# Down products of a feed-forward block as pairs of 64-row matmuls, their token tiles changing halves of the array behind a semaphore

## The chip, the cores and the metric

The kernel runs on one core of a Trainium2 chip. The metric is the device time of one execution in microseconds. The engines are TensorE (PE; its weight loads are shown apart as PEld), VectorE (DVE), ScalarE (ACT), GpSimd (POOL) and SyncE (SP), which issues the DMAs.

## What is computed

```python
def _A_ref(x, wqkv, wo):                       # 32 heads of 18
    qkv = (x @ wqkv).reshape(B, S, 3, H, Dh).transpose(2, 0, 3, 1, 4)
    scores = einsum("bhqd,bhkd->bhqk", q, k) * (Dh ** -0.5)
    o = einsum("bhqk,bhkd->bhqd", softmax(scores), v)
    return o.transpose(0, 2, 1, 3).reshape(B, S, D) @ wo

def _B_ref(x, w_gate, w_up, w_down):
    return (gelu(x @ w_gate) * (x @ w_up)) @ w_down

xn = layernorm(x)                              # x: 1 x 2048 x 576, float32
return x + _A_ref(xn, wqkv, wo) * silu(_B_ref(xn, w_gate, w_up, w_down))   # F = 4608
```

## The kernel before

A matrix product of float32 numbers is made of three products of split parts: each operand is cut into a high part and the rest (`h` and `l` in the names), and high x high, high x low and low x high are summed.

The 2048 tokens are four blocks `b` of 512. The feed-forward part walks over 36 sections per token block, 144 in all; a section makes 128 of the 4608 hidden units for 512 tokens. Its 27 pairs of matmuls (`gate_up`, L422) work on 64 rows each: `pg` in the upper half of the array's rows, `pu` in the lower half. Between these pairs stand the attention's score matmuls, also as pairs of 64 rows: `pm` (L809, for the running maximum) and `pe` (L855, whose exponential is taken by ScalarE in L856). VectorE reduces each `pm` (L810). After a section of the attention's stretch come the values (`acc`, L872, 128 rows by 32 columns of weights), and then, after every second section, a down block.

A down block multiplies the gated hidden units of two sections (256 of them, as `G` = 2 groups) with their rows of `w_down`. From the sixth block on it does so by seven products in place of eight (a Strassen scheme, `PRODUCTS`): the operands `ah`, `al` (`A`, hidden units by tokens) and `T` (sums of parts of `w_down`) hold seven combinations, and each product is added into one of the seven accumulators `M` by VectorE (L545; for `r` = 0 it is a copy). The first five blocks (`PLAIN`) use the four plain products, of six terms each (`down_plain`, L525). A product writes `py`, a tile of two PSUM banks: bank `t` holds 128 tokens by 288 columns. In each bank the three terms are three matmuls of 128 rows and 288 columns, so a seven-product block is 42 matmuls and a plain one 48.

`ring("py")` takes the next of three PSUM buffers (`RING`) of two banks each. `pm`, `pe`, `acc`, `py` and, in some sections, `pgu` go through this same ring in the order of the program, so each allocation waits until the reader of the third tile ahead of it has ended.

The order on TensorE and SyncE is as written; on the other engines a scheduler sets it, apart from what is marked `keep_in_program_order`. Down blocks are called in `downs`, one section late: block k after section 2k + 2. The last three (`last_down`) are in the closing part, where TensorE is also busy with the output projection.

Of the kernel before, what the change touches and what calls it, by code (L numbers as in the profile page):

```python
# [17 lines left out]
P = 128  # L18
# [5 lines left out]
HR = 64  # L24
# [13 lines left out]
G = 2  # L38
NR = F // (G * P)
NF = NB * NR * G  # L40
# [5 lines left out]
DC, TH = D // 2, TB // 2  # L46
ENDS = NF - len(FIRST) - NU * NA
# [5 lines left out]
PRODUCTS = ((2, (0, 6)), (5, (1, 3)), (3, (2, 5)), (6, (3, 4)), (0, (4, 2)), (4, (5, 1)), (1, (6, 0)))  # L53
# [35 lines left out]
def kernel(ctx: ExitStack, tc: tile.TileContext, x, wqkv, wo, w_gate, w_up, w_down, out):  # L89
    nc = tc.nc  # L90
    x = x.rearrange("b s d -> (b s) d")
# [80 lines left out]
    with tc.tile_pool(name="pro", bufs=1) as pro, tc.tile_pool(name="pps", bufs=1, space=PSUM) as pps:  # L172
# [156 lines left out]
        t = ORDER[0]  # L329
# [24 lines left out]
        for b in range(NB):  # L354
# [41 lines left out]
    FF = {"w": ahead, "xd": XD, "down": [], "gates": [], "n": 0, "hooks": {}, "raw": {},  # L396
          "M": ffn.tile([P, 7, 2, DC], F32, name="M"),
          "A": [ffn.tile([P, 7, TH], F32R, name=m) for m in ("ah", "al")],
          "T": ffn.tile([P, 2, 7, DC], F32R, name="T")}
# [4 lines left out]
    def ring(name):  # L404

        return ps.tile([P, 2, TB], F32, name=name, tag="ring", bufs=RING)
# [104 lines left out]
    def cut_plain_b(raw):  # L511
        T = FF["T"]
        cut(T[:, 0, 0:4], T[:, 1, 0:4], raw.rearrange("p g (c d) -> p (g c) d", c=2), nc.scalar, nc.gpsimd,
            tc.keep_in_program_order)

    def down_plain():
        (ah, al), T, M = FF["A"], FF["T"], FF["M"]
        for i, c, into in ((0, 0, ((6, ALU.add),)), (0, 1, ((2, ALU.add), (5, ALU.subtract))),
                           (1, 0, ((3, ALU.subtract), (6, ALU.subtract))), (1, 1, ((5, ALU.add),))):
            py = ring("py")  # L520
            terms = [(h, 2 * g + i, w, 2 * g + c) for g in range(G) for h, w in ((ah, 0), (ah, 1), (al, 0))]
            for t in range(2):
                tt = slice(t * P, (t + 1) * P)
                for n, (h, a, w, k) in enumerate(terms):
                    nc.tensor.matmul(py[:, t, 0:DC], h[:, a, tt], T[:, w, k], start=n == 0, stop=n == len(terms) - 1)  # L525
            for m, op in into:
                nc.vector.tensor_tensor(M[:, m], M[:, m], py[:, :, 0:DC], op=op)

    def down(b, r, then={}):
        if b == 0 and r < PLAIN:  # L530
            return down_plain()
        (ah, al), T, M = FF["A"], FF["T"], FF["M"]
        for m, (i, k) in PRODUCTS:
            py = ring("py")
            for t in range(2):
                tt = slice(t * P, (t + 1) * P)
                for n, (h, w) in enumerate(((ah, 0), (ah, 1), (al, 0))):
                    nc.tensor.matmul(py[:, t, 0:DC], h[:, i, tt], T[:, w, k], start=n == 0, stop=n == 2)  # L538
            if r == 0:
                if b == 1:  # L540
                    nc.vector.tensor_copy(M[:, m], py[:, :, 0:DC])
                else:
                    nc.scalar.activation(M[:, m], py[:, :, 0:DC], AF.Copy)
            else:
                nc.vector.tensor_tensor(M[:, m], py[:, :, 0:DC], M[:, m], op=ALU.add)  # L545
            for eng, to, op, by in then.get(m, ()):
                eng.tensor_tensor(M[:, to], M[:, to], M[:, by], op=op)
        if r == NR - 1 and b < NB - 1:
            FF["gates"].append(b)
            for k, (p, q) in enumerate(COMBINED):  # L550
                combine_at(6 * k + 6, nc.gpsimd, q)
                combine_at(6 * k + 6, nc.gpsimd, p)

    def combine_at(i, eng, what):
        FF["hooks"].setdefault(i, []).append(lambda: combine(eng, *what))
# [65 lines left out]
    def downs(then={}):  # L621
        while FF["down"] and (FF["down"][0][-1] < FF["n"] or FF["n"] == NF):
            down(*FF["down"].pop(0)[:-1], then)
# [125 lines left out]
    with tc.tile_pool(name="att", bufs=1, reuse_waits="tile") as att:  # L749
# [179 lines left out]
        for n in range(NU * NA):  # L929
            u, i = divmod(n, NA)  # L930
# [7 lines left out]
            if FF["n"] % G == 1 and SCALED <= n < NU * NA - 2 and 2 < FF["n"] % (NR * G) < NR * G - 2:  # L938
                done = scaled + gated
                if (scaled + 1) * NA + 4 < n:  # L940
                    jobs, k = (load_scale, scale, store_scale), scaled
                    scaled += 1
                else:
                    jobs, k = (load_gate, gate, store_gate), gated
# [20 lines left out]
    with tc.tile_pool(name="epi", bufs=1, reuse_waits="tile") as epi:  # L965
# [7 lines left out]
        n = 0  # L973
# [94 lines left out]
        def last_section(tag):  # L1068

            n = FF["n"]  # L1070
            FF["n"] += 1
            g = n % G
            pairs, pg, pu = gate_up(tag)
            hooks, FF["hooks"] = FF["hooks"], {}
            nxt = FF["raw"].pop(n + 1, None)
            if nxt:
                split_gu(nxt, 0)
                split_gu(nxt, 1)
            for t in spread(pairs, (), 1, hooks):
                t()  # L1080
            if nxt:
                split_gu(nxt, 2)
            FF["w"] = nxt
            h = ffn.tile([P, 3 + 3 * g, TH], F32, name=f"h{g}", bufs=2 - g)
            t1 = h[:, 0:2].rearrange("p a t -> p (a t)")

            def gelu():
                act.activation(t1, pg, AF.Square)
                vec.scalar_tensor_tensor(t1, t1, 1.0 / GC, pg, op0=ADD, op1=ALU.mult)
                act.activation(t1, t1, AF.Tanh, scale=GC * GS)  # L1090
                vec.scalar_tensor_tensor(t1, t1, 1.0, pg, op0=ADD, op1=ALU.mult)
# [16 lines left out]
        h, gelu = last_section("f")  # L1108
# [10 lines left out]
        h, gelu = last_section("ring")  # L1119
# [23 lines left out]
        for m in ("rawd", "tsum"):  # L1143
            t = ffn.tile([P, 2, D], F32, name="xxs", tag=m)
# [5 lines left out]
        h, gelu = last_section("ring")  # L1150
# [10 lines left out]
        M = FF["M"]  # L1161
# [17 lines left out]
        for i, c, m in QUARTERS:  # L1179
            t = ffn.tile([P, 2, DC], F32, name="tg", tag=("h0", "h1")[c], bufs=2 - c)  # L1180
# [34 lines left out]
```

## Time and profile before

| | |
|---|---|
| runs | 2544.12, 2545.7, 2547.68 us; median 2545.7 |
| profiled execution | span 2542.7 us (the profile gives its span alone) |
| TensorE matmuls | busy 2534.6 us (100% of the span), 20548 matmuls, granted clock 0.999 |
| TensorE weight loads | 1837.5 us (72%) |
| VectorE, ScalarE, GpSimd | 2092.2 us (82%), 1452.9 us (57%), 1620.2 us (64%) |
| chain that ended last | TensorE 97%, of which `py` L538 15% and `py` L525 1% |

In the profile's lines a form such as 64*128 64x512 is a weight tile of 64 rows by 128 columns and a moving operand of 64 rows by 512 columns. Starts of matmuls are recorded, their ends are modelled, and matmuls overlap: the distance between two starts tells what one of them takes from TensorE. In a timeline the columns are start, duration, engine, line, operation, tiles (out<-in), forms and count; what stands in brackets is the idle time of the engine ahead of the row and what ended it. In a list of waits they are total, number and longest, in us. In the chain they are start, length and what it was. A group's row gives its busy time, the mean of one in ns, and the idle time ahead with its causes.

### The profile page before, as it was taken

To read this page: it belongs to the slowest core of one execution; us is meant where nothing else is said; L and a number is where in the kernel's file an instruction comes from. 1 tells how busy PE (TensorE), PEld (TensorE's weight loads), DVE (VectorE), ACT (ScalarE), POOL (GpSimd) and SP (SyncE) were. 2 spreads that over 40 slices of the span, in tenths; PEclk is the share of its full clock that TensorE was granted. 3 is DMA by queue.
4 is the path that set the end of the run, shared out by engine and by line. 5 is a ranking of instruction groups with operands and counts; after the bars stand their busy time and mean duration, and the time that the engine had idled before them with its cause. 6 is when DMAs were issued, how large, how long until landed. Compare 5 with 4: busy or idle time off the path is not lost.

```text
span 2542.7 us, 53140 instructions
## 1 busy us (share of the span) xinstructions
PE 2534.6 (100%) x20548; PEld 1837.5 (72%) x20548; DVE 2092.2 (82%) x2371; ACT 1452.9 (57%) x1753; POOL 1620.2 (64%) x1684
## 2 busy tenths in 40 slices
PE   9999999999999999999999999999999999999999
PEld 8888866667766676666667666776666676667689
DVE  5327888889888888888897898998898888888357
ACT  3223466666666665556666555655566665556621
POOL 3005688888888876666658565666667666666773
PEclk9999999999999999999999999999999999999999
DMA  8965465555685565667787777666668666665676
GB/s 259 312 207 136 117 176 158 163 162 164 168 252 147 165 173 146 167 163 166 172 221 187 172 167 169 172 169 164 155 158 236 167 172 173 164 168 154 190 188 236
DMA packets 416627, 455.04 MB, mean 179 GB/s; under 512 B 109428, under 2 KB 289396, under 8 KB 416376
## 3 DMA queue, kind: packets, MB, share of 16 engines
q1 hardware_dynamic: 416376, 451.64, 66.3%
q8 instruction: 164, 2.69, 0.5%
q14 instruction: 87, 0.71, 0.1%
HBM read 354.38 MB, written 97.13 MB: 178 GB/s over the span
## 4 chain that ended last, share of the span: by engine, by line
PE 97%; DVE 1%; POOL 1%; issue 0%; DMA 0%; ACT 0%; SPq 0%; DVEq 0%; POOLq 0%
PE pg L422 25%; PE acc L872 18%; PE py L538 15%; PE pm L809 9%; PE pe L855 9%; PE pu L422 9%; PE po L193 6%; PE po L1026 2%; PE pgu L422 2%; PE py L525 1%; PE pt L263 0%; POOL M L560 0%; DVE KA L756 0%; DMA xx<-in_A_x_dram 0%; DMA KA<-qk 0%
## 5 line engine op out<-in xcount | busy, mean ns | idle before, releaser
L856 ACT ACTIVATE pT<-pe 128x1024 f32<-128x1024 f32 x1024 | 1048.2, 1027 | 580.3 <-PE pe L855 544.5
L810 DVE TENSOR_REDUCE mx<-pm 128x2 f32<-128x1024 f32 x1024 | 1219.4, 1224 | 162.3 <-PE pm L809 145.7
L422 PE MATMUL pu<-xd,wh 64*128 64x512 f32 x2466 | 901.7, 396 | 0.0
L422 PE MATMUL pg<-xd,wh 64*128 64x512 f32 x2466 | 901.2, 396 | 0.0
L422 PEld LDWEIGHTS pg<-xd,wh 64*128 64x128 f32 x2466 | 454.5, 184 | 113.5 <-issue 55.4
L117 POOL TENSOR_SCALAR wh<-raw 128x384 fp32r<-128x384 f32 x402 | 211.8, 530 | 456.8 <-PE pu L422 275.3
L422 PE MATMUL pg<-xd,wl 64*128 64x512 f32 x1233 | 480.9, 390 | 0.3 <-POOL wl L124 0.3
L422 PE MATMUL pu<-xd,wl 64*128 64x512 f32 x1233 | 481.0, 390 | 0.0
L422 PEld LDWEIGHTS pu<-xd,wh 64*128 64x128 f32 x2466 | 454.3, 184 | 18.7
L872 PE MATMUL acc<-pT,VS 128*32 128x512 f32 x4096 | 466.0, 595 | 0.0
L119 POOL TENSOR_TENSOR wl<-raw,wh 128x384 fp32r<-128x384 f32 x402 | 422.4, 1054 | 26.4
L809 PE MATMUL pm<-KA,QT 64*128 64x512 f32 x2048 | 410.9, 393 | 0.4 <-ACT pT L856 0.3
L855 PE MATMUL pe<-QT,KA 64*128 64x512 f32 x2048 | 409.0, 391 | 0.3 <-DVE mx L810 0.3
L538 PE MATMUL py<-T,ah 128*128 128x288 f32 x1876 | 380.6, 298 | 0.0
L545 DVE TENSOR_TENSOR M<-py,M 128x576 f32<-128x576 f32 x448 | 338.8, 758 | 31.4 <-PE py L538 18.2
L538 PEld LDWEIGHTS py<-T,ah 128*128 128x128 f32 x1876 | 298.3, 188 | 54.0 <-issue 54.0
L451 POOL TENSOR_TENSOR al<-h,ah 128x512 fp32r<-128x512 f32 (+1 forms) x143 | 295.3, 2065 | 51.6 <-ACT ah L448 37.9
L872 PEld LDWEIGHTS acc<-pT,VS 128*32 128x32 f32 x4096 | 120.2, 109 | 276.6 <-issue 229.6
L538 PE MATMUL py<-T,al 128*128 128x288 f32 x938 | 275.6, 294 | 0.0
L855 PEld LDWEIGHTS pe<-QT,KA 64*128 64x128 f32 x2048 | 191.9, 184 | 110.8 <-DVE mx L810 25.5
L422 PEld LDWEIGHTS pg<-xd,wl 64*128 64x128 f32 x1233 | 227.3, 184 | 33.8 <-POOL wl L124 0.7
L422 PEld LDWEIGHTS pu<-xd,wl 64*128 64x128 f32 x1233 | 227.5, 185 | 10.4
(167 smaller groups left out, 2943.5 us busy)
## 6 DMA issues: line engine op xcount, KB each, us to landing
T<-ts SPq DMA_DIRECT2D x98, 576.0 KB
KA<-qk SPq DMA_DIRECT2D x768, 72.0 KB
T<-ts SPq DMA_DIRECT2D x98, 432.0 KB
raw<-in_B_w_gate_dram SPq DMA_DIRECT2D x144, 288.0 KB
raw<-in_B_w_up_dram SPq DMA_DIRECT2D x144, 256.0 KB
ts<-T SPq DMA_DIRECT2D x36, 576.0 KB
VS<-vs SPq DMA_DIRECT2D x128, 152.0 KB
qk<-t SPq DMA_DIRECT2D x72, 256.0 KB
```

The lines of the kernel that those rows point to most:

```text
L117: first = nc.gpsimd.tensor_scalar(hi, raw, 1.0, 1.0, op0=ALU.mult, op1=ALU.mult)
L119: keep(nc.gpsimd.tensor_tensor(lo, raw, f(hi), op=ALU.subtract))
L193: nc.tensor.matmul(o, st, m, start=(i == 0), stop=(i == len(terms) - 1))
L422: nc.tensor.matmul(o, w[1 + wp][k][rr, c, :], xd[k][xp][rr, c, :], start=(i == 0), stop=(i == len(terms) - 1))
L451: low = two.tensor_tensor(lo, raw, f(hi), op=ALU.subtract)
L538: nc.tensor.matmul(py[:, t, 0:DC], h[:, i, tt], T[:, w, k], start=n == 0, stop=n == 2)
L545: nc.vector.tensor_tensor(M[:, m], py[:, :, 0:DC], M[:, m], op=ALU.add)
L809: nc.tensor.matmul(pm[:, a], QS[u, r][rr, t * P:(t + 1) * P], KS[(u * NA + c) % KB][r][rr, :], start=True, stop=True)
L810: nc.vector.tensor_reduce(MX[u][:, 2 * r:2 * r + 2, t, c], pm, axis=AX.X, op=ALU.max)
L855: nc.tensor.matmul(pe[:, a], KS[(u * NA + c) % KB][r][rr, t * P:(t + 1) * P], QS[u, r][rr, :], start=True, stop=True)
L856: nc.scalar.activation(PT[u, kt][:, 2 * r:2 * r + 2, :], pe, AF.Exp, scale=SCALE)
L872: nc.tensor.matmul(ACC[u][32 * a:32 * a + 32, :], VS[(u * NA + c) % VB][:, v:v + 32], pt[:, a, :], start=first, stop=last, skip_group_chec ...
```

## The change

`halved` takes a list of products. Each product is done in two phases of 64-row matmuls. In phase 0 the upper 64 rows of the operands go to the first token tile (bank 0) while the lower 64 rows go to the second (bank 1); in phase 1 the token tiles change halves. So each bank gets all 128 rows, from one half of the array after the other. Phase 1 of a product stands behind phase 0 of the next product. The last matmul of phase 0 adds one to the semaphore `turns`, and the first of phase 1 waits for it.

All down blocks but those of the last sections use it: 68 of the 72, of which five are plain. The old loop stays for the other four.

```diff
+    def halved(jobs):
+        (ah, al), T = FF["A"], FF["T"]
+        begun = []
+
+        def phase(py, terms, x, turn=0):
+            for n, (h, a, w, k) in enumerate(terms):
+                for half in range(2):
+                    t, rr = half ^ x, slice(HR * half, HR * half + HR)
+                    one = nc.tensor.matmul(py[:, t, 0:DC], h[rr, a, t * P:(t + 1) * P], T[rr, w, k], start=x == 0 and n == 0,
+                                           stop=x == 1 and n == len(terms) - 1)
+                    if x == 1 and n == half == 0:
+                        one._wait_ge(turns, turn)
+            if x == 0:
+                TURN["n"] += 1
+                one.then_inc(turns, 1)
...
+        def turned():
+            py, terms, then, turn = begun.pop(0)
+            phase(py, terms, 1, turn)
+            then(py)
+
+        for n, (terms, then) in enumerate(jobs):
+            py = ring("py")
+            phase(py, terms, 0)
+            begun.append((py, terms, then, TURN["n"]))
+            if n > 0:
+                turned()
+        turned()
...
     def down(b, r, then={}):
...
-        for m, (i, k) in PRODUCTS:
-            py = ring("py")
-            for t in range(2):
-                tt = slice(t * P, (t + 1) * P)
-                for n, (h, w) in enumerate(((ah, 0), (ah, 1), (al, 0))):
-                    nc.tensor.matmul(py[:, t, 0:DC], h[:, i, tt], T[:, w, k], start=n == 0, stop=n == 2)
+        def take(py, m):
...
+        terms = ((ah, 0), (ah, 1), (al, 0))
+        if FF["n"] < NF - ENDS:
+            halved([([(h, i, w, k) for h, w in terms], lambda py, m=m: take(py, m)) for m, (i, k) in PRODUCTS])
+        else:
+            for m, (i, k) in PRODUCTS:
+                py = ring("py")
+                for t in range(2):
+                    tt = slice(t * P, (t + 1) * P)
+                    for n, (h, w) in enumerate(terms):
+                        nc.tensor.matmul(py[:, t, 0:DC], h[:, i, tt], T[:, w, k], start=n == 0, stop=n == 2)
+                take(py, m)
```

`down_plain` calls `halved` in the same way with its four products of six terms.

On TensorE, a seven-product block begins like this before (each `py` number is one product's tile; a wait for DVE_49 is one for VectorE):

```order
L538 MATMUL py_19123<-T_1917,ah_1915 128x288 [waits DMAHW1_49,PE_49]
L538 MATMUL py_19123<-T_1917,ah_1915 128x288 [waits DMAHW6_49]
L538 MATMUL py_19123<-T_1917,al_1916 128x288
L538 MATMUL py_19123<-T_1917,ah_1915 128x288 x2
L538 MATMUL py_19123<-T_1917,al_1916 128x288
L538 MATMUL py_19131<-T_1917,ah_1915 128x288 [waits DVE_49]
L538 MATMUL py_19131<-T_1917,ah_1915 128x288
L538 MATMUL py_19131<-T_1917,al_1916 128x288
```

On TensorE in the changed kernel, from the second product's first phase to the fourth's:

```order
L528 MATMUL py_19886<-T_1917,ah_1915 128x288 [waits DVE_49]
L528 MATMUL py_19886<-T_1917,ah_1915 128x288 x3
L528 MATMUL py_19886<-T_1917,al_1916 128x288 x2
L528 MATMUL py_19879<-T_1917,ah_1915 128x288 [waits turns]
L528 MATMUL py_19879<-T_1917,ah_1915 128x288 x3
L528 MATMUL py_19879<-T_1917,al_1916 128x288 x2
L528 MATMUL py_19900<-T_1917,ah_1915 128x288 [waits DVE_49,Pool_49]
...
L528 MATMUL py_19886<-T_1917,ah_1915 128x288 [waits turns]
...
L528 MATMUL py_19914<-T_1917,ah_1915 128x288 [waits DVE_49]
```

The first product (19879) is finished behind the first phase of the second (19886), and the fourth (19914), which takes the first one's buffer, begins six steps of two matmuls behind that, where twelve matmuls stood between them before.

On TensorE, a block's last rows in the changed kernel:

```order
L528 MATMUL py_19956<-T_1917,ah_1915 128x288 [waits DVE_49]
L528 MATMUL py_19956<-T_1917,ah_1915 128x288 x3
L528 MATMUL py_19956<-T_1917,al_1916 128x288 x2
L528 MATMUL py_19942<-T_1917,ah_1915 128x288 [waits turns]
L528 MATMUL py_19942<-T_1917,ah_1915 128x288 x3
L528 MATMUL py_19942<-T_1917,al_1916 128x288 x2
L528 MATMUL py_19956<-T_1917,ah_1915 128x288 [waits turns]
L528 MATMUL py_19956<-T_1917,ah_1915 128x288 x3
L528 MATMUL py_19956<-T_1917,al_1916 128x288 x2
```

The last two products end three steps apart, and the seventh waits for `turns` with only the sixth's second phase between. Every other matmul on TensorE stands in the same order as before, and SyncE's order is the same. The other engines run the same instructions; GpSimd's and ScalarE's order differs by a few places, and on VectorE the first addition of a plain block stands behind one activation step instead of ahead of it.

More of the change, by code (lines that the diff above doesn't have):

```diff
@@ L514, in cut_plain_b @@
             tc.keep_in_program_order)
+    turns = tc.alloc_semaphore("turns")
+    TURN = {"n": 0}
+    def halved(jobs):
[12 more added lines that the diff above has]
+                one.then_inc(turns, 1)
+                tc.no_tile_sem_insts.add(one.ins.name)
+                tc.add_to_no_dep_group(f"turn{TURN['n']}", one.ins)
+            else:
+                tc.declare_fence(one.ins, group=f"turn{turn}")
+        def turned():
[9 more added lines that the diff above has]
+        turned()
@@ L516, in down_plain, with add_to @@
     def down_plain():
-        (ah, al), T, M = FF["A"], FF["T"], FF["M"]
+        (ah, al), M = FF["A"], FF["M"]
+        jobs = []
         for i, c, into in ((0, 0, ((6, ALU.add),)), (0, 1, ((2, ALU.add), (5, ALU.subtract))),
                            (1, 0, ((3, ALU.subtract), (6, ALU.subtract))), (1, 1, ((5, ALU.add),))):
-            py = ring("py")
-            terms = [(h, 2 * g + i, w, 2 * g + c) for g in range(G) for h, w in ((ah, 0), (ah, 1), (al, 0))]
-            for t in range(2):
-                tt = slice(t * P, (t + 1) * P)
[L524 to L527, printed above, removed]
+            def add_to(py, into=into):
+                for m, op in into:
+                    nc.vector.tensor_tensor(M[:, m], M[:, m], py[:, :, 0:DC], op=op)
+            jobs.append(([(h, 2 * g + i, w, 2 * g + c) for g in range(G) for h, w in ((ah, 0), (ah, 1), (al, 0))], add_to))
@@ L529, in down @@
+        halved(jobs)
     def down(b, r, then={}):
@@ L532, in down @@
         (ah, al), T, M = FF["A"], FF["T"], FF["M"]
-        for m, (i, k) in PRODUCTS:
-            py = ring("py")
-            for t in range(2):
-                tt = slice(t * P, (t + 1) * P)
-                for n, (h, w) in enumerate(((ah, 0), (ah, 1), (al, 0))):
-                    nc.tensor.matmul(py[:, t, 0:DC], h[:, i, tt], T[:, w, k], start=n == 0, stop=n == 2)
+        def take(py, m):
             if r == 0:
@@ L547, in down @@
                 eng.tensor_tensor(M[:, to], M[:, to], M[:, by], op=op)
+        terms = ((ah, 0), (ah, 1), (al, 0))
+        if FF["n"] < NF - ENDS:
+            halved([([(h, i, w, k) for h, w in terms], lambda py, m=m: take(py, m)) for m, (i, k) in PRODUCTS])
+        else:
+            for m, (i, k) in PRODUCTS:
[5 more added lines that the diff above has]
+                take(py, m)
         if r == NR - 1 and b < NB - 1:
```

## The prediction

> **What bounds the kernel now.** I read the page first (busy shares and the chain that ended last), then the waits of TensorE, then the timeline of one down block on TensorE, its weight loads and VectorE.
>
> ```profile
> span 2542.7 us, 53140 instructions
> PE 2534.6 (100%) x20548; PEld 1837.5 (72%) x20548; DVE 2092.2 (82%) x2371; ACT 1452.9 (57%) x1753; POOL 1620.2 (64%) x1684
> PE 97%; DVE 1%; POOL 1%; issue 0%; DMA 0%; ACT 0%; SPq 0%; DVEq 0%; POOLq 0%
> PE pe L855 <- DVE mx L810: 0.3, 1, 0.3
> PE pm L809 <- ACT pT L856: 0.3, 1, 0.3
> PE pg L422 <- POOL wl L124: 0.3, 1, 0.3
> ```
>
> TensorE is the chain for 97%, and the three waits shown are one of 0.3 us each. Any time that TensorE gains or loses therefore shows in full. The next view is one down block (42 matmuls) between the values and the next section.
>
> ```profile
> 1003.48 0.53 PE L538 MATMUL py<-T,ah 128*128 128x288 f32 x2
> 1003.85 0.29 PE L538 MATMUL py<-T,al 128*128 128x288 f32 x1
> ...
> 1004.24 0.29 PE L538 MATMUL py<-T,al 128*128 128x288 f32 x1
> ...
> 1008.99 0.29 PE L538 MATMUL py<-T,al 128*128 128x288 f32 x1
> 1009.21 0.49 PE L422 MATMUL pg<-xd,wh 64*128 64x512 f32 x1
> ...
> 1009.55 0.40 PE L855 MATMUL pe<-QT,KA 64*128 64x512 f32 x2
> ...
> 1010.02 0.39 PE L809 MATMUL pm<-KA,QT 64*128 64x512 f32 x2
> ...
> 1010.72 0.40 PE L855 MATMUL pe<-QT,KA 64*128 64x512 f32 x2
> ...
> 1011.88 0.39 PE L855 MATMUL pe<-QT,KA 64*128 64x512 f32 x2
> ...
> 1019.08 0.39 PE L422 MATMUL pg<-xd,wh 64*128 64x512 f32 x1
> ```
>
> Starts matter here, since matmuls overlap. From the third matmul (1003.85) to the 42nd (1008.99) are 39 steps in 5.14 us: 0.132 us a step. From the second pair of the section (1009.55) to its 43rd (1019.08) are 41 pairs in 9.53 us: 0.232 us a pair of 512 columns. Between the last down matmul and the second pair lie 0.56 us where 0.132 + 0.232 = 0.36 would do: leaving the 128-row shape costs 0.20 us.
>
> VectorE beside it, with the means of its two largest jobs:
>
> ```profile
> 1004.57 0.76 DVE L545 TENSOR_TENSOR M<-py,M 128x576 f32<-128x576 f32 x1 [0.26 <-PE py L538]
> 1010.48 1.23 DVE L810 TENSOR_REDUCE mx<-pm 128x2 f32<-128x1024 f32 x1 [0.40 <-PE pm L809]
> L545 DVE TENSOR_TENSOR M<-py,M 128x576 f32<-128x576 f32 x448 | 338.8, 758 | 31.4 <-PE py L538 18.2
> ```
>
> The last matmul of the first product starts at 1004.24 and VectorE takes the product at 1004.57: 0.33 us, then 0.758 us. Seven takes need 5.3 us of the 42 x 0.132 = 5.5 us, so VectorE is nearly as full as TensorE there.
>
> What a late wait costs shows where the pm pair at 1756.46 waited for ScalarE:
>
> ```profile
> 1755.38 1.02 ACT L856 ACTIVATE pT<-pe 128x1024 f32<-128x1024 f32 x1 [2.31 <-PE pu L422]
> 1756.46 0.50 PE L809 MATMUL pm<-KA,QT 64*128 64x512 f32 x2
> 1756.79 0.40 PE L422 MATMUL pg<-xd,wh 64*128 64x512 f32 x1
> 1756.46 0.19 PEld L809 LDWEIGHTS pm<-KA,QT 64*128 64x128 f32 x2 [0.27 <-ACT pT L856]
> 1756.57 0.19 PEld L422 LDWEIGHTS pg<-xd,wh 64*128 64x128 f32 x1
> ```
>
> ScalarE ends at 1756.40; the waiting pair's weight loads begin only 0.06 us later, together with it, and the next pair follows after 0.33 instead of 0.232 us. A wait thus holds back the load as well: to lose nothing, a buffer must be free 0.06 + 0.10 = 0.16 us before the matmul that takes it.
>
> **The change part by part.** Of 72 down blocks, 68 are halved: 5 plain ones (48 steps) and 63 of seven products (42 steps); the block before the last three and those three stay.
>
> *Matmuls.* Each 128-row matmul becomes two 64-row ones, one in each half of the rows. They run beside each other, as pg with pu: that pair of 512 columns takes 0.232 us. Scaled to 288 columns it is 0.130 us, the old step 0.132. I take 0.132, so 0 (from -6 us for 2886 steps of 0.130). Upwards the nearest row is the densest stream of loads and matmuls that the trace has, 32 of each in 3.57 us:
>
> ```profile
> 999.98 3.57 PE acc L872 x32
> 1003.55 5.74 PE py L538 x42
> 1009.55 0.18 PEld L422 LDWEIGHTS pg<-xd,wl 64*128 64x128 f32 x1
> 1009.56 0.18 PEld L422 LDWEIGHTS pu<-xd,wl 64*128 64x128 f32 x1
> ```
>
> That is 0.112 us for one load and one matmul, so two of each are at most 0.223 us: the upper end. I stay at 0.132, since the acc matmuls have more columns (512) and their own work may set that spacing, while the pairs are of the new shape. The two loads of a pair start together at 1009.55, while the pair before (also 1009.55) streams through the same halves, and so are hidden. The Trainium skill (TensorE: Matmul & The Clock Gate, "The mechanism") says that loads overlap running matmuls only when their row groups differ; by that rule every halved step would pay its load too, about 0.1 us and some 300 us in all. The trace disagrees with it, by those rows.
>
> *Changes of shape.* Downs and sections now have the same shape, so the 0.20 us on leaving a block go: 63 x 0.20 = 12.4 us. Entering from acc (128 rows by 32 columns) stays a change. A plain block follows a section directly, and its entry goes too:
>
> ```profile
> 216.99 0.39 PE L422 MATMUL pg<-xd,wh 64*128 64x512 f32 x1
> ...
> 217.30 0.53 PE L525 MATMUL py<-T,ah 128*128 128x288 f32 x2
> 217.67 0.29 PE L525 MATMUL py<-T,al 128*128 128x288 f32 x1
> ```
>
> From pair to third matmul are 0.68 us where 0.232 + 2 x 0.132 = 0.50 would do. 5 x (0.20 + 0.18) = 1.9 us. Sum: -14.2 us.
>
> *The ring.* Call the first half of a product F, the second S. The new order is F0 F1 S0 F2 S1 F3 S2 F4 S3 F5 S4 F6 S5 S6, three steps each. Three ring buffers serve it, so F3 needs what take 0 frees. Before, 13 steps (1.72 us) lay between the last matmul of a product and the first of the third product behind it; 0.33 + 0.758 + 0.16 = 1.25 us are needed, 0.47 to spare. Now S0, F2, S1, F3 leave 7 steps, 0.92 us: short by 0.32. Step by step, from the block's first matmul: S0's last matmul is at 1.06, take 0 runs 1.39 to 2.15, F3 starts at 2.31 instead of 1.98. Take 1 runs 2.18 to 2.94 and F4 is due at 3.10, just in time. S2 comes late by 0.32, so take 2 ends at 4.05, and F5 starts at 4.21 instead of 3.89; F6 is just in time again. Two late waits, 0.65 us a block, 63 blocks: +40.9 us. Nobody else is behind this on TensorE but the whole queue, and nothing covers it. In plain blocks a phase has six steps: 13 again, none late.
>
> *After the block.* The next section starts (P0) 6.19 us after the block's first matmul; takes 5 and 6 end 0.56 and 1.32 us behind P0 (before: take 6 at 0.76). P0 of before is 1009.55 - 0.232 = 1009.32; its first pm stands at +0.70, second pe at +1.40, third pe at +2.56. They need takes 5 and 6 and the first reduction: +0.72, +1.48, and, since that reduction starts at 1.32 instead of 1.16 and takes 1.23, +2.71. Each late wait moves the rest: 0.02 + 0.06 + 0.07 = 0.15 us. Bounds: 0 (VectorE a little quicker) and 0.30 (one more reduction late). 63 x 0.15 = +9.5 us.
>
> *The semaphore turns.* S waits for F of its own product. Closest are S0 and S6: F's last matmul, then three steps, so the load is wanted 3 x 0.132 = 0.40 us after that matmul's start; the end of a py matmul shows at 0.29, VectorE saw it at 0.33, and 0.06 us more for the release on TensorE make 0.35 to 0.39. Just in time: 0. If not, two loads a block come late.
>
> *Other queues.* VectorE, ScalarE and GpSimd have the same instructions. In plain blocks take 0 moves behind one activation step; its buffer is not wanted until step 30. GpSimd's splits stand a few places otherwise; TensorE waited once, 0.3 us, for them. The T loads are issued after the block as before. 0 for all.
>
> Sum: -14.2 + 40.9 + 9.5 = +36.2 us on a span of 2542.7, so 2578.9. The median of the runs (2545.7) lies 3.0 us above that span: 2581.9, put at 2582.
>
> **The rivals.**
>
> *Only the change of shape counts* (the other side). If F3 and F5 do not wait, the time is 2545.7 - 14.2 = 2531.5. It needs takes about 0.3 us shorter, or free of the 0.16; it decides once the stalls of a block stay below 14.2 / 63 = 0.23 us. For it: the sum rests on a margin that no row of before shows used up in a down. Against: both durations are measured, and the shortfall, 0.32, is a third of the interval.
>
> *TensorE cannot issue so densely.* Two loads and two matmuls in 0.132 us are shown nowhere. At 0.223 a step 2886 steps cost +263 us, the ring no longer binds, and the time is 2545.7 - 14.2 + 263 = 2794; midway (0.178) 2886 x 0.046 = 133 us, 7 steps just reach 1.25 us, 2665. The Trainium skill (the same page, "Back-to-back issue gap") gives about 81 ns for a sustained load and matmul of 128 columns: a step of 0.162, by which I estimate about 2640. No run here shows that row.
>
> *turns comes late.* If a completion is seen 0.1 to 0.2 us later by TensorE itself, S0 and S6 each lose that: 63 x 0.2 to 0.4 = 13 to 25 us more, 2595 to 2607.
>
> **How the numbers follow.** The ring 72%, its own range 2565 to 2600 (a late wait of 0.2 to 0.42 us; 0 to 0.3 us after the block); change of shape alone 10%; issue 8%; turns 10%. The time is the ring's, 2582. The range 2558 to 2612 takes in ring and turns and leaves out the other two, 18%. About 0.2%, 5 us, is what a measurement here tells from no change. Faster: 9 of the second case's 10. Same: its rest and the low tail of the ring, 3. Slower: 88.
>
> **What would show it.** In the after trace: steps within a half-phase at 0.132 us; no gap beyond 0.36 us between block and section; the fourth and sixth F of each block waiting for VectorE M, about 126 waits, with their loads starting together with them and 0.1 us more behind; a block in the chain at about 6.2 us against 5.74 with its shape change; VectorE without idle time between takes. Wrong would be: steps clearly above 0.132 with no wait (issue), waits at S rather than F (turns), or F without waits (faster).

## The result, and the profile after

The changed kernel takes 2591.19 us (median of four runs, 2590.51 to 2592.28) against 2545.93 us for the kernel before on the same chip (four runs, 2544.12 to 2547.68): a ratio of 1.0179, interval 1.0166 to 1.0193. It is slower by 45 us, where 36 us were predicted.

First the page of the changed kernel: span, busy time, and the chain that ended last by engine and by line.

```profile
span 2588.7 us, 58893 instructions
PE 2564.9 (99%) x23434; PEld 1873.9 (72%) x23434; DVE 2082.3 (80%) x2371; ACT 1453.9 (56%) x1753; POOL 1617.5 (62%) x1684
PE 89%; DVE 6%; DMA 2%; POOL 2%; issue 1%; ACT 0%; SPq 0%; POOLq 0%; DVEq 0%
PE pg L422 26%; PE acc L917 17%; PE py L528 12%; PE pm L854 9%; PE pe L900 9%; PE po L193 6%; PE pu L422 5%; DVE M L578 3%; PE po L1071 2%; PE pgu L422 1%; DMA raw<-in_B_w_up_dram 1%; DVE mx L855 1%; PE py L591 1%; POOL wl L119 1%; DMA xd<-xhs 0%
```

TensorE had 97% of the chain and now has 89%; VectorE went from 1% to 6%, and its taking of products (`M` L578) is a line of the chain with 3%. The list of waits tells where (total, number, longest):

```profile
PE pe L900 <- DVE mx L855: 7.2, 5, 2.9
PE py L528 <- DVE M L561: 1.9, 3, 1.1
PEld py L528 <- DVE M L578: 35.3, 120, 0.3
```

The third row is the ring: 120 waits for a take, 0.29 us each. It stands under the weight loads and not under the matmuls, because the modelled end of the matmul before covers most of so short a gap. Whoever reads the rows of TensorE's matmuls alone doesn't find it. The first two rows are waits that the prediction did not have.

One block on the timeline of the changed kernel follows, TensorE first; the last row of that list, at 1056.17, is where the next block ends. The single row behind it is the same place in the kernel before. Then come VectorE's takes and the weight loads at the first wait, again in the changed kernel:

```profile
1016.05 0.54 PE L528 MATMUL py<-T,ah 64*128 64x288 f32 x4
...
1018.00 0.30 PE L528 MATMUL py<-T,al 64*128 64x288 f32 x2
1018.36 0.53 PE L528 MATMUL py<-T,ah 64*128 64x288 f32 x4
1018.73 0.29 PE L528 MATMUL py<-T,al 64*128 64x288 f32 x2
...
1019.93 0.29 PE L528 MATMUL py<-T,al 64*128 64x288 f32 x2
1020.28 0.53 PE L528 MATMUL py<-T,ah 64*128 64x288 f32 x4
...
1022.24 0.29 PE L528 MATMUL py<-T,al 64*128 64x288 f32 x2
1022.36 0.39 PE L422 MATMUL pg<-xd,wh 64*128 64x512 f32 x1
...
1022.60 0.40 PE L900 MATMUL pe<-QT,KA 64*128 64x512 f32 x2
...
1056.17 0.40 PE L422 MATMUL pg<-xd,wh 64*128 64x512 f32 x1
```

```profile
1042.47 0.49 PE L422 MATMUL pg<-xd,wh 64*128 64x512 f32 x1
```

```profile
1017.55 1.55 DVE L578 TENSOR_TENSOR M<-py,M 128x576 f32<-128x576 f32 x2 [0.67 <-PE py L528]
1019.47 1.55 DVE L578 TENSOR_TENSOR M<-py,M 128x576 f32<-128x576 f32 x2 [0.37 <-PE py L528]
```

```profile
1018.36 0.30 PEld L528 LDWEIGHTS py<-T,ah 64*128 64x128 f32 x4 [0.30 <-DVE M L578]
```

From 1018.00 to 1018.36 lies one step that should be 0.132 us, and F3 at 1018.36 begins just behind the first take (1017.55, half of 1.55, so to 1018.32). Its loads begin with it, so the step after it is long too: from 1018.36 to 1018.73 are two steps in 0.37 where 0.264 would do. F5 at 1020.28 repeats this behind the third take. The block then ends without a seam: 0.12 to 0.13 us to the section's first pair (1022.24 to 1022.36) and 0.23 to its second, where 0.22 and 0.34 stood before.

From one block's end to the next is 33.81 us (1022.36 to 1056.17), against 33.26 before (1009.21 to 1042.47): 0.55 more here. Measured on the first gate/up pairs of all 144 sections in both traces, the time from the section ahead of a block to the section behind it grew by 0.58 us in nearly all of the 63, and the section behind kept its length. (Below, a section's number stands for the section with the block behind it, where there is one.) That is 36.5 of the 46.0 us by which the span grew. Of the rest, 8.9 us lie in two places alone: sections 74 and 110 (in the third and fourth token block) grew by 5.01 us each, 4.43 more than the others.

In the trace of the changed kernel, section 74 waits here, GpSimd first, then VectorE and TensorE:

```profile
1375.41 0.52 POOL L117 TENSOR_SCALAR wh<-raw 128x384 fp32r<-128x384 f32 x1
...
1377.59 1.01 POOL L119 TENSOR_TENSOR wl<-raw,wh 128x384 fp32r<-128x384 f32 x1
1378.56 1.28 POOL L462 TENSOR_TENSOR h<-h,h 128x512 f32<-128x512 f32 x1
1379.79 0.19 POOL L864 CAST m<-nm 128x16 fp32r<-128x16 f32 x1
...
1380.62 0.22 POOL L865 TENSOR_TENSOR m<-nm,m 128x16 fp32r<-128x16 f32 x1
```

```profile
1380.87 0.21 DVE L870 STREAM_TRANSPOSE mt<-m 128x32 f32<-128x32 f32 x1 [2.95 <-POOL m L865]
```

```profile
1382.25 0.50 PE L900 MATMUL pe<-QT,KA 64*128 64x512 f32 x2 [2.78 <-DVE mx L855]
```

And GpSimd at the same place in the kernel before:

```profile
1354.36 1.37 POOL L119 TENSOR_TENSOR wl<-raw,wh 128x384 fp32r<-128x384 f32 x1
1355.69 1.29 POOL L462 TENSOR_TENSOR h<-h,h 128x512 f32<-128x512 f32 x1
1356.92 0.20 POOL L819 CAST m<-nm 128x16 fp32r<-128x16 f32 x1
```

Two more pairs of weight splits (L117 and L119, 3.2 us from 1375.41 to 1378.56) stand ahead of the two small `m` operations. VectorE's transpose waits for these in its own order, the reductions `mx` stand behind the transpose, and TensorE stands behind a reduction.

The wait is not all that the stall costs. Behind it TensorE is slow:

```profile
1383.39 0.63 PE L854 MATMUL pm<-KA,QT 64*128 64x512 f32 x2
1383.82 0.62 PE L422 MATMUL pg<-xd,wl 64*128 64x512 f32 x1
```

These two pairs stand 0.43 us apart, where 0.232 is the rule. The trace has TensorE's granted clock at 0.50 of full speed from 1382.62 to 1386.03 us, and again from 1997.02 to 2000.43 behind the stall of section 110. Up to its values, section 74 took 4.60 us more than before: 2.94 are the wait, 0.10 the late load of the waiting pair, and some 1.55 the 3.41 us at the low clock.

### The profile page after: what moved, and what is told of

Its sections match the earlier page's. It is cut to its first block, busy times and chain, and to the rows that moved or that the text cites. A ratio compares the mean times of both kernels' runs of the same rounds, so it can differ in the third digit from the quotient of the medians.

```text
span 2588.7 us, 58893 instructions
## 1 busy us (share of the span) xinstructions
PE 2564.9 (99%) x23434; PEld 1873.9 (72%) x23434; DVE 2082.3 (80%) x2371; ACT 1453.9 (56%) x1753; POOL 1617.5 (62%) x1684
## 4 chain that ended last, share of the span: by engine, by line
PE 89%; DVE 6%; DMA 2%; POOL 2%; issue 1%; ACT 0%; SPq 0%; POOLq 0%; DVEq 0%
PE pg L422 26%; PE acc L917 17%; PE py L528 12%; PE pm L854 9%; PE pe L900 9%; PE po L193 6%; PE pu L422 5%; DVE M L578 3%; PE po L1071 2%; PE pgu L422 1%; DMA raw<-in_B_w_up_dram 1%; DVE mx L855 1%; PE py L591 1%; POOL wl L119 1%; DMA xd<-xhs 0%
## 5 line engine op out<-in xcount | busy, mean ns | idle before, releaser
L117 POOL TENSOR_SCALAR wh<-raw 128x384 fp32r<-128x384 f32 x402 | 216.2, 538 | 491.9 <-PE pu L422 253.3
L119 POOL TENSOR_TENSOR wl<-raw,wh 128x384 fp32r<-128x384 f32 x402 | 413.8, 1030 | 32.8
L900 PE MATMUL pe<-QT,KA 64*128 64x512 f32 x2048 | 422.0, 394 | 7.2 <-DVE mx L855 7.2
L854 PE MATMUL pm<-KA,QT 64*128 64x512 f32 x2048 | 426.3, 396 | 0.4 <-ACT pT L901 0.3
L528 PE MATMUL py<-T,ah 64*128 64x288 f32 x3848 | 408.8, 302 | 9.1 <-DVE M L561 1.9
L578 DVE TENSOR_TENSOR M<-py,M 128x576 f32<-128x576 f32 x448 | 333.1, 756 | 92.9 <-PE py L528 83.9
L528 PEld LDWEIGHTS py<-T,ah 64*128 64x128 f32 x3848 | 303.4, 184 | 92.9 <-issue 52.8
L528 PE MATMUL py<-T,al 64*128 64x288 f32 x1924 | 285.7, 291 | 0.0
L854 PEld LDWEIGHTS pm<-KA,QT 64*128 64x128 f32 x2048 | 211.4, 185 | 46.2 <-DVE M L578 11.6
```

Source lines behind the costliest of these rows:

```text
L117: first = nc.gpsimd.tensor_scalar(hi, raw, 1.0, 1.0, op0=ALU.mult, op1=ALU.mult)
L119: keep(nc.gpsimd.tensor_tensor(lo, raw, f(hi), op=ALU.subtract))
L528: one = nc.tensor.matmul(py[:, t, 0:DC], h[rr, a, t * P:(t + 1) * P], T[rr, w, k], start=x == 0 and n == 0, stop=x == 1 and n == len(terms ...
L854: nc.tensor.matmul(pm[:, a], QS[u, r][rr, t * P:(t + 1) * P], KS[(u * NA + c) % KB][r][rr, :], start=True, stop=True)
L900: nc.tensor.matmul(pe[:, a], KS[(u * NA + c) % KB][r][rr, t * P:(t + 1) * P], QS[u, r][rr, :], start=True, stop=True)
```

## The experiments

Theory: the ring (two late takes a block) makes the 0.58 us, and GpSimd's order makes the stalls in sections 74 and 110. Rivals for the first: the halved matmuls themselves, or the waits for `turns`. For the second: anything else that comes late there, since the two `m` operations had only been seen to stand behind the splits.

**The order alone.** Whole 128-row matmuls in the new order, no halves and no semaphore.

```diff
             for n, (h, a, w, k) in enumerate(terms):
-                for half in range(2):
-                    t, rr = half ^ x, slice(HR * half, HR * half + HR)
-                    one = nc.tensor.matmul(py[:, t, 0:DC], h[rr, a, t * P:(t + 1) * P], T[rr, w, k], start=x == 0 and n == 0,
-                                           stop=x == 1 and n == len(terms) - 1)
-                    if x == 1 and n == half == 0:
-                        one._wait_ge(turns, turn)
-            if x == 0:
-                TURN["n"] += 1
-                one.then_inc(turns, 1)
...
+                nc.tensor.matmul(py[:, x, 0:DC], h[:, a, x * P:(x + 1) * P], T[:, w, k], start=n == 0, stop=n == len(terms) - 1)
```

> 128-row matmuls as before, but in the changed kernel's order: first token tile of a product, first tile of the next, then second tile of the product; no semaphore, no halves. Ring theory: the fourth and the sixth product of a block wait 0.33 us each for VectorE as in the changed kernel, 63 x 0.65 = +41 us; the change of shape on leaving a block (0.20 us) stays, and because the section then starts 0.20 us later VectorE has caught up and nothing is lost behind the block. GpSimd's order is the one of before around the block changes, so no 5 us stalls there. 2545.9 + 41 = 2587 us. Rival (the halves themselves, or their semaphore, cost the time): 2546 us.

Measured: 2586.72 us, ratio 1.0164 (1.0149 to 1.0179). The same two steps of each block are late. TensorE at F3:

```profile
1019.68 0.29 PE L526 MATMUL py<-T,al 128*128 128x288 f32 x1
1020.02 0.53 PE L526 MATMUL py<-T,ah 128*128 128x288 f32 x2
1020.39 0.29 PE L526 MATMUL py<-T,al 128*128 128x288 f32 x1
```

By the median over the blocks the late step is 0.354 and the next 0.238 us at F3, 0.345 and 0.238 at F5; in the changed kernel 0.361, 0.238, 0.351 and 0.238. A block and its section grow by 0.66 us. So the order is the loss, with halves or without; halves and semaphore add nothing within the block. That it is the order by way of the ring, the next run shows. Sections 74 and 110 grow by 0.46 and 0.44 us only, and GpSimd's order there is that of before: the 5 us belong to how the halved kernel is scheduled, not to the ring.

**Shorter takes.** VectorE takes half of the columns of the seven products (the other half is left out).

```diff
-                nc.vector.tensor_tensor(M[:, m], py[:, :, 0:DC], M[:, m], op=ALU.add)
+                c = slice(0, DC // 2)
+                nc.vector.tensor_tensor(M[:, m, :, c], py[:, :, c], M[:, m, :, c], op=ALU.add)
```

> The changed kernel with VectorE's additions of the seven products over half of their columns only (144 of 288 in each bank; the other half of the sums is left out). Ring theory: a take is about 0.38 us instead of 0.758, so 0.33 + 0.38 + 0.16 = 0.87 us fit into the 0.92 us of seven steps, no wait in the blocks and none behind them: 2545.9 - 14.2 = 2531.7, and with the two stalls of about 4.4 us at the start of the third and fourth token block, which come from GpSimd's order and stay, 2541 us. Rival (halves or semaphore cost the time): 2580 to 2591 us.

Measured: 2555.15 us, ratio 1.0039 (1.0024 to 1.0054), 14 us above what was expected. The group of takes, and the largest wait of TensorE:

```profile
L579 DVE TENSOR_TENSOR M<-py,M 128x288 f32<-128x288 f32 x448 | 201.0, 458 | 152.9 <-PE py L528 143.8 <-PE py L592 9.1
PE pe L901 <- DVE mx L856: 12.8, 11, 3.8
```

A take is 0.458 us, and by the median the two late steps are 0.126 and 0.132 us with 0.168 and 0.164 behind them: 0.03 us is left of each wait, as 0.33 + 0.458 + 0.16 = 0.95 us against the 0.92 of seven steps would have it. A block with its two sections is 0.13 us shorter than before, not longer. The miss is elsewhere: sections 74 and 110 grew by 6.03 and 5.79 us, and eight others (38, 58, 70, 82, 98, 102, 114, 118) by 0.7 to 1.1, some 19 us in all. It is one cause: in each of the ten VectorE's transpose stands idle (0.57 to 1.04 us in the eight, 3.97 and 3.63 in 74 and 110) and begins 0.03 us behind the second `m` operation on GpSimd. Behind both long stalls the granted clock is 0.50 for 3.41 us, as in the changed kernel. So the blocks confirm the ring, and GpSimd's order costs more than the 8.9 us that were expected of it.

**The two `m` operations on VectorE**, so that GpSimd's splits cannot stand ahead of them.

```diff
-            keep(nc.gpsimd.tensor_copy(m2[:, :, 0], n2))
-            keep(nc.gpsimd.tensor_tensor(m2[:, :, 1], n2, f(m2)[:, :, 0], op=SUB))
+            keep(nc.vector.tensor_copy(m2[:, :, 0], n2))
+            keep(nc.vector.tensor_tensor(m2[:, :, 1], n2, f(m2)[:, :, 0], op=SUB))
```

> The changed kernel with the two small operations that split the running maximum moved from GpSimd to VectorE. Theory: the two sections that grew by 5.0 us instead of 0.6 did so because VectorE waited in order for these two operations, which in GpSimd's new order stand behind two more weight splits; with them on VectorE these sections grow by 0.6 like the others, minus 8.9 us: 2582 us. Rival (those stalls have another cause, such as transfers at the start of a token block): 2591 us.

Measured: 2597.89 us, ratio 1.0215 (1.0197 to 1.0232): neither of the two. The groups of the moved operations, and TensorE's largest wait:

```profile
L864 DVE CAST m<-nm 128x16 fp32r<-128x16 f32 x32 | 27.3, 854 | 1.1
L865 DVE TENSOR_TENSOR m<-nm,m 128x16 fp32r<-128x16 f32 x32 | 24.1, 753 | 1.1
PE pe L900 <- DVE accs L923: 17.8, 24, 1.1
```

Sections 74 and 110 fall to +0.55 and +0.45 us, so the stall there is indeed a wait for these two. But on VectorE they take 0.85 and 0.75 us in the mean, where GpSimd took 0.20 and 0.22, and 24 other sections go from +0.58 to between +1.45 and +2.04 us. (The profiled execution, at 2606.77 us, is 8 to 10 us longer than the other three, so these are somewhat large.)

The means hide two cases. Six times out of 32 the two took 0.18 to 0.24 and 0.17 to 0.18 us; the other 26 times each was running beside a GpSimd instruction and ended 0.02 to 0.04 us behind that one's end, after 0.73 to 1.24 and 0.43 to 1.22 us. At the start of sections 38, 74, 90, 110 and 114 they were short, and none of these sections grew by more than 0.70 us. So it is not that VectorE is slow at small operations: beside GpSimd's work they wait for its end. The cure costs more than the illness, and the time alone would have spoken for the wrong theory.

**A fourth buffer.** The gate and up sums become one tile of two banks, and the fourth product of a block uses it.

```diff
-            pg, pu = (ps.tile([P, TB], F32, name=n, tag=tag, bufs=2) for n in ("pg", "pu"))
+            two = ps.tile([P, 2, TB], F32, name="pf", tag=tag, bufs=1)
+            pg, pu = two[:, 0], two[:, 1]
...
-            py = ring("py")
+            py = ps.tile([P, 2, TB], F32, name="py", tag="f", bufs=1) if n == 3 and len(jobs) == 7 else ring("py")
```

> The changed kernel with a fourth PSUM buffer for the fourth product of each block: the two banks of the gate and up sums (pg, pu), which nobody uses during a block, as one tile. Ring theory: 13 steps or more lie between the end of each product and the next use of its buffer, as before the change, so no wait in the blocks; the seventh take still ends 1.3 us into the next section, 0.15 us lost there, and GpSimd's order and its two stalls stay: 2545.9 - 14.2 + 9.5 + 8.9 = 2550 us. Rival (halves or semaphore): about 2590 us.

Measured: 2566.72 us, ratio 1.0082 (1.0065 to 1.0098), 17 us above. The waits of TensorE:

```profile
PE pe L901 <- DVE mx L856: 15.2, 11, 4.8
PE py L529 <- DVE M L562: 5.1, 5, 1.7
```

By the median neither F3 nor F5 is late any more, and 33 of the 63 blocks are now shorter than before, most by about 0.12 us, so the buffer does cure the ring. But sections 74 and 110 grow by 6.66 and 5.87 us (with the granted clock at 0.50 behind both stalls), six others by 0.8 to 1.75 where VectorE again waits for the `m` operations, the plain sections' waits are 5.1 us together (second row), and in the first half every second block is 0.36 us longer: a wait that this kernel adds, and the run with the three cures, below, shows where.

**The wait for `turns` with nothing to cover it.**

```diff
-            if n > 0:
-                turned()
-        turned()
+            turned()
```

> The change with one thing undone: the second half-phase of a product is issued right behind its own first half-phase (F0 S0 F1 S1 ...), with no half-phase of a neighbour between, so the semaphore's wait has nothing to cover it. It prices the wait that the changed kernel hides. In the changed kernel's trace a matmul that is let go by another engine loses about 0.33 us to the next step. If a wait on PE's own semaphore costs the same, 63 blocks x 7 x 0.33 + 5 sections x 4 x 0.33 = +152 us; the ring then needs nothing more (the takes are spaced wider), so the 41 us of the ring's waits go: 2591 + 152 - 41 = about 2700 us, between 2650 and 2740. If PE's own increments come back within a step (0.13 us) the turns cost nothing even so, and the time stays by 2550 to 2591 us.

Measured: 2682.59 us in one run, beside 2546.47 for the kernel before. TensorE at one of these waits:

```profile
1052.97 0.30 PE L528 MATMUL py<-T,al 64*128 64x288 f32 x2
1053.33 0.53 PE L528 MATMUL py<-T,ah 64*128 64x288 f32 x4
1053.70 0.29 PE L528 MATMUL py<-T,al 64*128 64x288 f32 x2
```

By the median the first step of a second phase is 0.358 us and the next 0.239: 0.333 us lost per product, 2.33 us per block, of which the change of shape gives a part back: block and section are 2.2 us longer than before. The late load shows for 0.107 us here as for 0.106 behind VectorE's take; that the whole losses, 0.333 and 0.335, are alike too is chance, since F3's also depends on how late the take is. By these numbers I estimate that a second phase goes at full pace if 0.358 + 0.107 = 0.465 us lie between the start of the last matmul of the first phase and its own; in the changed kernel there are four steps, 0.528 us. The `turns` are covered, with 0.06 us to spare. (The ring's wait is gone here, since the takes are spaced wider.)

**GpSimd's order.** The changed kernel, but with the weight splits of one section per token block, the one that forms the next maxima, held to the order of the program.

```diff
+        if FF.pop("pin", False):
+            one = lambda hi, lo, raw: split(hi, lo, raw, keep)
...
+            FF["pin"] = FF["n"] > ATT.start
```

> The changed kernel with one thing pinned: in the one section per token block that forms the next maxima (n = 37, 73, 109), GpSimd's weight splits keep the program's order, so that the two GpSimd operations for which VectorE's transpose waits stand ahead of the two split pairs as they do in the kernel before. Theory: the 5.01 us by which sections 74 and 110 grew are that order, so each falls to about +0.6 and the time to 2591.2 - 2 x 4.4 = about 2582 us (ratio about 1.0145). Rival: something else makes PE wait there, and the time stays by 2591.

Measured: 2579.12 us, ratio 1.0129 (1.0114 to 1.0145): 12 us less than the changed kernel, where 9 were expected. GpSimd and VectorE at the place of the stall:

```profile
1376.09 0.21 POOL L866 CAST m<-nm 128x16 fp32r<-128x16 f32 x1
```

```profile
1377.20 0.21 DVE L872 STREAM_TRANSPOSE mt<-m 128x32 f32<-128x32 f32 x1 [0.52 <-POOL m L867]
```

The transpose waits 0.52 instead of 2.95 us, sections 74 and 110 go from +5.01 to +1.09 and +0.37, the granted clock stays at 1.00 through them, and the blocks keep their 0.58. That is 8.6 us; 2.9 more come from sections 36, 38, 78 and 118, which had grown by 1.1 to 1.3 us in the changed kernel and now stand at 0.04 to 0.59. In three of these (38, 78, 118) the transpose had waited 0.4 to 1.0 us for GpSimd's `m`. This settles the second part.

**The three cures together, and one more.** The fourth buffer, the splits in order, and the plain sections as before:

```diff
     def down_plain():
-        halved(jobs)
+            for t in range(2):
+                tt = slice(t * P, (t + 1) * P)
+                for n, (h, a, w, k) in enumerate(terms):
+                    nc.tensor.matmul(py[:, t, 0:DC], h[:, a, tt], T[:, w, k], start=n == 0, stop=n == len(terms) - 1)
```

> Three edits on the changed kernel: the fourth product of each block takes its accumulation tile from the two banks of the gate/up sums (a fourth buffer in the ring), the splits are pinned as in e6_splits_in_order, and the five plain sections are as in the kernel before. If all that the change costs is the ring's wait of 0.58 us per block and the stalls of GpSimd's order, what is left is the gain at the turn from a block to a section, 63 x 0.2 = 12.6 us, less up to 0.15 us per block that VectorE loses behind it: 2536 to 2543 us (ratio 0.996 to 0.999). The rival, that the fourth buffer delays the next section's gate and up sums by as much as it saves: 2545 to 2560.

Measured: 2549.46 us, ratio 1.0012 (1.0004 to 1.0021): the rival's range, not the theory's, though not for the rival's reason. Blocks of -0.12 us alternate with blocks of +0.25 to +0.4. In a long one, VectorE and ScalarE, then TensorE:

```profile
1035.59 0.68 DVE L433 SCALAR_TENSOR_TENSOR h<-h,pf 128x512 f32<-128x512 f32 x1
...
1037.72 1.26 DVE L440 SCALAR_TENSOR_TENSOR h<-h,t 128x512 f32<-128x512 f32 x1
1038.91 0.68 DVE L927 TENSOR_TENSOR accs<-acc,accs 128x512 f32<-128x512 f32 x1
```

```profile
1036.30 0.60 ACT L436 ACTIVATE t<-pf 128x512 f32<-128x512 f32 x1 [1.01 <-DVE h L433]
```

```profile
1039.30 0.30 PE L529 MATMUL py<-T,al 64*128 64x288 f32 x2
1039.73 0.54 PE L529 MATMUL py<-T,ah 64*128 64x288 f32 x4
```

F2 at 1039.73 takes the buffer that `acc` had, and VectorE frees it at 1038.91 + 0.68 = 1039.59: 0.30 us late. VectorE may come to it late because ScalarE's copy of the up sums waited 1.01 us for VectorE's first read of the gate sums: they are one tile now, and the two readings are ordered. (The last run tests this.) Sections 74 and 110 stand at +0.78 and +0.96.

The same with the first transposes and combinations of the section behind a block placed one to three products later:

```diff
+    if first == 2:
+        at = [1, 3, 5, 6, 8, 10, 12, 13, 15, 17, 19, 20, 22, 24, 26, 26]
```

> As e7_fourth_buffer_plain_back, and in the sections behind a block the first transposes and combinations of activations are placed one to three products later, so that VectorE's last take of the block and the section's first operations do not fall together. If the 0.15 us per block behind the block is VectorE's backlog, it goes: 2533 to 2540 us, 3 to 9 us below e7_fourth_buffer_plain_back. If moving them later makes the section's last activations late instead: 2545 to 2570.

Measured: 2556.66 us, ratio 1.0042 (1.0030 to 1.0055), 7 us worse than without. The blocks are as in the run before, but the sections behind a block, the very ones that were changed, lose some 0.12 us each. This is the second of the two outcomes that were named; that it is the last activations which come late was not shown.

And the run with the three cures, without these later places but with ScalarE's copy placed ahead of VectorE's first read:

```diff
         nc.scalar.activation(t1, pg, AF.Square)
-        nc.vector.scalar_tensor_tensor(t1, t1, 1.0 / GC, pg, op0=ALU.add, op1=ALU.mult)
         if early:
             t2 = ffn.tile([P, TB], F32, name="t2", bufs=1)
             nc.scalar.activation(t2, pu, AF.Copy)
+        nc.vector.scalar_tensor_tensor(t1, t1, 1.0 / GC, pg, op0=ALU.add, op1=ALU.mult)
+        if early:
             nc.vector.tensor_tensor(t2, t2, pg, op=ALU.mult)
```

> As e7_fourth_buffer_plain_back, with one line moved: ScalarE's copy of the up sums stands ahead of VectorE's first read of the gate sums. In e7_fourth_buffer_plain_back gate and up sums are one tile, and the copy waited for that read (ScalarE 1036.301 behind VectorE 1035.588 + 0.679), which put VectorE's add of accs at 1038.907 to 1039.585 and with it the third half-phase of every second block at 1039.731, 0.30 us late. Theory: the copy's wait is what makes accs late; with the copy first, accs come about 0.27 us earlier, most of the 0.30 us in every second block goes, and the time falls by 5 to 9 us to 2540 to 2545 us, below the kernel before. Rival: what makes accs late is VectorE's h, which took 1.261 us there and 0.692 us in the next block (beside GpSimd's split), and the time stays at 2547 to 2552 us.

Measured: 2536.76 us against 2544.71 before on that chip, ratio 0.9967 (0.9955 to 0.9979): faster than both kernels. VectorE from the h to the takes of a block, and the block's end on TensorE:

```profile
1032.81 1.38 DVE L441 SCALAR_TENSOR_TENSOR h<-h,t 128x512 f32<-128x512 f32 x1
1034.11 0.68 DVE L928 TENSOR_TENSOR accs<-acc,accs 128x512 f32<-128x512 f32 x1
1035.23 5.37 DVE L580 TENSOR_TENSOR M<-py,M 128x576 f32<-128x576 f32 x7 [0.45 <-PE py L530]
```

```profile
1033.74 0.54 PE L530 MATMUL py<-T,ah 64*128 64x288 f32 x4
...
1039.37 0.40 PE L423 MATMUL pf<-xd,wh 64*128 64x512 f32 x2
```

Relative to the block's first matmul, `accs` starts at 0.37 instead of 0.77 us, although the h before it still took 1.38 us. So the long h alone does not make `accs` late. It has its part: in the run with the three cures the block ahead of the one shown had an h of 0.69 us, `accs` started at 0.19 us, and nothing was late. The seven takes now stand back to back, 5.37 us, and the block with its change of shape takes 5.63 us (1033.74 to 1039.37) against 5.73 before and 6.31 in the changed kernel. Each block with its sections is about 0.11 us shorter than before, 63 x 0.11 = 7 of the 8.0 us between the medians. In the profiled execution, with 2540.89 us the longest of the six, sections 72, 74 and 110 give back 1.0, 2.4 and 1.3 us; in the last two VectorE's transpose still waits for GpSimd's `m`, 1.9 and 1.3 us.

## Why the prediction was right, and where not

*The ring: right.* Two late waits a block, F3 and F5, at 0.32 us each were predicted. The steps show 0.229 + 0.106 at F3 and 0.219 + 0.106 at F5, 0.66 us a block: 41.6 us where 40.9 stood in the sum. The order alone gives the same, and with takes of 0.458 us it is gone.

*The step of 0.132 us: right.* Within the phases the median is 0.132, so two loads and two matmuls go through in that time and the rival of issue is out. By the Trainium skill (TensorE: Matmul & The Clock Gate, "Back-to-back issue gap") the estimate was 0.162 a step, and by "The mechanism" of the same page the loads would have been paid for; neither held for these pairs, of 288 columns.

*The change of shape: right.* Last step 0.132 and next 0.231 us, where 0.222 and 0.335 stood: 0.19 us a block, 12 us.

*After the block: right in kind, somewhat less.* With 0.66 lost in the block and 0.19 won at its end, the 0.58 us leave 0.11 for what lies behind it, against 0.15. That is a remainder; no run measured it alone. The prediction also put the section's start 6.19 us behind the block's first matmul; it is 6.31, since the first step of a block, behind the values, is 0.24 and not 0.132 us.

*The `turns`: right.* Nothing was lost; the margin is 0.06 us, estimated from the run that lays the wait bare.

*"Other queues ... 0 for all": wrong.* This is the term that failed. "GpSimd's splits stand a few places otherwise; TensorE waited once, 0.3 us, for them" looked at who waits for the splits, and not at what stands behind them in GpSimd's own order. Two pairs of splits ahead of the `m` operations cost 2 x 4.43 us through VectorE's transpose, of which about 3 us each are the wait and 1.5 the low clock behind it, and smaller stalls in a few other sections; holding the splits in order takes 12 us away. The same paragraph's "its buffer is not wanted until step 30" failed too, by little: the list of waits has three waits of 1.9 us together for the plain sections' take L561, and the sections of the five plain blocks, put at -1.9 us, came out 0.7 us longer. The forecast range had room for the 9 us that the sum lacked.

*"VectorE without idle time between takes": wrong.* It stands idle 0.37 us ahead of the second pair of takes in the block shown, and takes come in pairs. The prediction's own steps said so (a late F3 makes S2 and its take late); the sentence did not follow them. When both wait for each other in turn, both show gaps, and neither looks full.

The rival on the other side, change of shape alone at 2531.5 us, is what the last kernel comes near to: 2536.8, once no product waits for a take.

## What to carry to other kernels

When phases of neighbouring products are interleaved, two accumulations are open at once, and a ring that was deep enough loses a place: count the steps between a product's last matmul and the first matmul that takes its buffer, and compare them with the hand-over at both ends and the take. A wait of a third of a microsecond hides in the row of the weight loads. Where a schedule moves instructions on a side engine by a few places, go through what stands behind them there and who waits for that, not only through who waits for the moved ones. And read a mean beside its single values: 0.85 us in the mean was 0.2 in some places and 1.2 in others, and the difference was the cause.

## What the runs showed of the hardware

A stall of TensorE costs more than its length if it is long. In the changed kernel and in the runs with short takes and with the fourth buffer, six times 3.2 to 5.2 us lay between the starts of two pairs, and each time the granted clock was 0.50 for the next 3.41 us and a pair of 512 columns took about 0.42 us. In the other runs the longest such distance in the feed-forward part was 2.1 us, and the clock stayed at 1.00 there.

A matmul let go by TensorE's own semaphore started 0.358 us behind the start of the one that it waited for, and the step behind it took 0.239 us in place of 0.132, as behind a matmul let go by VectorE (0.238).

VectorE's h of 128x512 took 1.26 and 1.38 us in the blocks shown, while its other operations of that size took 0.68. In the last kernel GpSimd ran a split at that time:

```profile
1032.63 1.00 POOL L119 TENSOR_TENSOR wl<-raw,wh 128x384 fp32r<-128x384 f32 x1
```

The split ends at 1033.63, and the h, begun at 1032.81, ends 0.56 us after that: it looks as if it did next to nothing until GpSimd was done. The whole trace of that kernel bears it out. Of its 139 such h, the 84 that started with no GpSimd instruction running took 0.68 to 0.69 us; of the 55 others, all but one ended 0.54 to 0.64 us behind the end of that instruction, after up to 1.45 us. The small `m` operations on VectorE showed the same. The Trainium skill (SBUF — State Buffer, "SBUF: two separate sides") has the two engines share one pair of ports, which one holds for its whole instruction, against operations with two inputs from SBUF among others; these rows agree with it, though no run took the split away from beside the h.
